# Sink keys in two transfers, limits and slopes on another queue, early weights one at a time

## The chip, the cores and the metric

The kernel runs on one core of a Trainium2 chip. The metric is the device time of one execution in microseconds (us). Engines: TensorE (PE), VectorE (DVE), ScalarE (ACT), GpSimd (POOL), and SyncE (SP), whose queue issues transfers.

## The reference

Windowed attention with a few always visible first keys ("sinks"), then two dense blocks on all 1536 rows:

```python
B, H, S, D = 2, 8, 768, 64              # n_sink = 4, window = 128
scores = q @ k.T / sqrt(D)
keep = (key < n_sink) | ((0 <= row - key) & (row - key < window))
a = softmax(where(keep, scores, -1e9))
x = (a @ v)                             # to [B*S, H*D] = [1536, 512]
x = (silu(x @ w_gate) * (x @ w_val)) @ w_out          # d_ff 1536
h = x @ w_in                                          # d_ff 2048
out = (max(h, 0) + alpha * min(h, 0)) @ moe2_w_out
```

`n_sink` and `window` are inputs, so the masks are built on the chip. All of it has to be accurate: each matmul of the dense blocks is three matmuls on a high and a low part.

## The kernel before, in words

Attention is cut into 24 groups (`Group`). A group is one sequence, two heads (a head pair, `hp`) and two blocks of 128 rows. The first eight groups (`ORDER`, `NPASS`) give the first 512 rows of x; none of them has a sink block apart from the window. The sixteen groups after them run beside the first experts' work. A group goes through stages: `load` (keys and queries, four transfers), `load_v` (values, two), `prep` (transposes on TensorE, ScalarE copies them to `th`), `scores` (matmuls; VectorE adds the mask and takes the bound `nb`; ScalarE takes the exponential and its sum), `norm` (VectorE the reciprocal `rinv`, GpSimd the product), `flip` (transposes of the probabilities), `values` (matmuls, and the split into xh and xl). `attention` (L364) writes these in software-pipelined order: iteration x has scores of group x, values of x-2, flip of x-1, norm of x, prep of x+2, load of x+3, load_v of x+1.

Ahead of iteration 0, `begin_a` builds the identity and loads `n_sink` and `window` (`limits`, L75), `begin_b` builds the masks and loads and prepares the slopes alpha (`slopes`, L92; 2048 single values of 4 bytes). At the end of iterations 0 and 1 `sink_load` (L350) asks for the first 32 keys of all heads of a sequence in four transfers, at the end of iterations 2 and 3 `sink_keys` (L358) transposes them into `kst`.

A group with sinks keeps the probabilities of a block as 128 window columns and 32 sink columns (`KW` = 160), with the sinks behind in the first block and ahead in the second. `norm` multiplies the window columns of both blocks in one GpSimd operation and the sinks in two, into `sk`, which a transpose (L320) turns for the value matmuls.

Expert weights come as 64-bit values, 512 KB a piece. `Stream.load` asks for one (three raw buffers, `RB`), `convert` makes a high and a low part with two ScalarE and four VectorE operations, and `tick` (L597) does one of each. While the first eight groups run, `tick` is called at the flips until two weights are converted (`EARLY`, L851); after that, one step of the first expert unit and one `tick` follow each 2300 units of attention's cost. The unit goes through the gate matmuls (pg), the value matmuls (pv) and the output matmuls (po).

The order in which instructions are written gives priorities; a planner with a simulated timeline then orders the instructions of each engine and each queue, and may draw one ahead when its engine would be idle. All transfers are issued on SP's queue, in order, and one issue waits there for its buffer to come free.

Of the kernel before, what the change touches and what calls it, by code (L numbers as in the profile page):

```python
# [16 lines left out]
P = 128  # L17
# [17 lines left out]
WB = 13  # L35
WX = 6
RB = 3
VB = 4
ORDER = ((0, 3), (1, 2), (4, 5))
EARLY = 2  # L40
WEAVE = 2300
NG = 2
# [32 lines left out]
def limits(nc, g, n_sink, window):  # L75
    lim = []
    for nm, src in (("ns", n_sink), ("wd", window)):
        raw = g.const.tile([P, 2], I32, name=nm + "_raw")
        nc.sync.dma_start(out=raw, in_=src.bitcast(I32).partition_broadcast(P))
        lo = g.const.tile([P, 1], F32, name=nm + "_lo")  # L80
        nc.vector.tensor_copy(lo, raw[:, 0:1].bitcast(U32))
        hi = g.const.tile([P, 1], F32, name=nm + "_hi")
        nc.vector.tensor_copy(hi, raw[:, 1:2])
        v = g.const.tile([P, 1], F32, name=nm + "_v")
        nc.vector.scalar_tensor_tensor(
            out=v, in0=hi, scalar=4294967296.0, in1=lo, op0=ALU.mult, op1=ALU.add
        )
        lim.append(v)
    g.ns, g.wd = lim


def slopes(nc, g, alpha):  # L92
    nc.sync.dma_start(out=g.alpha, in_=alpha.rearrange("(f p) -> p f", p=P))
    nc.vector.tensor_scalar(out=g.sig, in0=g.alpha, scalar1=1.0, scalar2=-2.0, op0=ALU.is_gt, op1=ALU.mult)
    nc.vector.tensor_scalar(out=g.sig, in0=g.sig, scalar1=1.0, scalar2=None, op0=ALU.add)
    nc.vector.tensor_tensor(out=g.sal, in0=g.alpha, in1=g.sig, op=ALU.mult)
    nc.vector.tensor_scalar(out=g.sdn, in0=g.sig, scalar1=DOWN, scalar2=None, op0=ALU.mult)
# [34 lines left out]
def attention_pools(nc, tc, ctx, g):  # L132
    for nm, bufs in (("raw_p", 2), ("tr_p", 3), ("pr_p", 3), ("pt_p", 2), ("st_p", 4)):
        setattr(g, nm, ctx.enter_context(tc.tile_pool(name=nm, bufs=bufs)))
    g.nb = g.const.tile([P, B * H * NQ], F32, name="nb")
    g.wsum = g.const.tile([P, NW], F32, name="wsum")
    g.ksr = [g.const.tile([NPAIR * SINK, 2 * D], F32, name="ksr") for _ in range(B)]
    g.kst = [g.const.tile([P, NPAIR * SINK], F32, name="kst") for _ in range(B)]
    g.vsr = g.const.tile([4 * SINK, NPAIR, NG, 2 * D], F32, name="vsr")
    nc.gpsimd.memset(g.vsr, 0.0)  # L140


class Group:
# [109 lines left out]
            )  # L253

    def prb_at(self, t):
        return 2 * self.blocks(0)[0] if t else 0

    def pr(self, t, e, c, n):
        w = self.blocks(t)[0]
# [3 lines left out]
    def norm(self):  # L263
        nc, g = self.nc, self.g
        rinv = g.st_p.tile([P, NG, 2], F32, tag="rinv", name="rinv")
        nc.vector.tensor_scalar(out=rinv, in0=self.ssum, scalar1=EPS, scalar2=None, op0=ALU.add)
        nc.vector.reciprocal(out=rinv, in_=rinv)
        for c, n, dst in ((0, P, None), (1, SINK, "sk")) if self.sink else ((None, 0, None),):
            if c is None:
                for t in range(NG):  # L270
                    w = self.blocks(t)[0]
                    o = self.prb_at(t)
                    v = self.prb[:, o:o + 2 * w].rearrange("p (e w) -> p e w", e=2)
                    r = rinv[:, t].unsqueeze(2).to_broadcast([P, 2, w])
                    nc.gpsimd.tensor_tensor(out=v, in0=v, in1=r, op=ALU.mult)
                continue
            offs = []
            for t in range(NG):
                w, blk, sp, kk = self.blocks(t)
                offs.append(self.prb_at(t) + (sp if c else blk[0]))  # L280
            step = offs[1] - offs[0]
            v = self.prb[:, offs[0]:offs[0] + 2 * step].rearrange("p (t w) -> p t w", t=NG)
            if step >= 2 * KW:
                v = v[:, :, :2 * KW].rearrange("p t (e w) -> p t e w", e=2)[:, :, :, :n]
                parts = [(v, slice(0, NG))]
            else:
                parts = [
                    (self.prb[:, o:o + 2 * KW].rearrange("p (t e w) -> p t e w", t=1, e=2)[:, :, :, :n], slice(t, t + 1))
                    for t, o in enumerate(offs)
                ]  # L290
            if dst:
                self.sk = g.pr_p.tile([P, NG, 2, SINK], F32, tag="sk", name="sk")
            for v, ts in parts:
                r = rinv[:, ts].unsqueeze(3).to_broadcast([P, ts.stop - ts.start, 2, n])
                nc.gpsimd.tensor_tensor(out=self.sk[:, ts] if dst else v, in0=v, in1=r, op=ALU.mult)

    def flip(self, t):
        nc, g = self.nc, self.g
        w, blk, sp, kk = self.blocks(t)
        if t == 0:  # L300
            self.pt = g.pt_p.tile([P, 2, 2 * NG, P], F32, tag="pt", name="pt")
        nb = len(blk)
        ps = g.ps_t.tile([P, 512], F32, tag="ps", name="ps_p")
        for e in range(2):
            for x, c in enumerate(blk):
                y = (e * nb + x) * P
                nc.tensor.transpose(ps[:, y:y + P], self.pr(t, e, c, P), g.ident)
        b0 = max(0, 2 * t - self.off)
        psv = ps[:, :2 * nb * P].rearrange("p (e c) -> p e c", e=2)
        if sp is None:  # L310
            nc.scalar.activation(self.pt[:, :, b0:b0 + nb].rearrange("p e a c -> p e (a c)"), psv, AF.Copy)
        else:
            nc.vector.tensor_tensor(
                out=self.pt[:, :, b0:b0 + 2], in0=psv.unsqueeze(2).to_broadcast([P, 2, 2, P]),
                in1=g.tri.unsqueeze(1).to_broadcast([P, 2, 2, P]), op=ALU.mult,
            )
        if t == NG - 1 and self.sink:
            self.pts = g.pt_p.tile([P, P], F32, tag="pts", name="pts")
            ps = g.ps_t.tile([P, 512], F32, tag="ps", name="ps_p2")
            nc.tensor.transpose(ps[:, 0:P], self.sk.rearrange("p t e s -> p (t e s)"), g.ident)  # L320
            nc.scalar.activation(self.pts, ps[:, 0:P], AF.Copy)

    def values(self):
# [24 lines left out]


def sink_load(nc, g, k, b):  # L350
    for hp in range(NPAIR):
        nc.sync.dma_start(
            out=g.ksr[b][hp * SINK:(hp + 1) * SINK].rearrange("p (e d) -> p e d", e=2),
            in_=k[b, 2 * hp:2 * hp + 2, 0:SINK, :].rearrange("h p d -> p h d"),
        )


def sink_keys(nc, g, b):  # L358
    ps = g.ps_t.tile([P, 512], F32, tag="ps", name="ps_ks")
    nc.tensor.transpose(ps[:, :P], g.ksr[b], g.ident)  # L360
    nc.scalar.activation(g.kst[b], ps[:, :P], AF.Copy)


def attention(groups, begin):  # L364
# [15 lines left out]
    for x in range(n + 2):  # L380
        if x < n:
            for t in range(NG):
                groups[x].scores(t)
            yield 1200, None
        if x >= 2:
            for c in groups[x - 2].values():
                yield c, None
            yield 0, groups[x - 2]
        if 1 <= x <= n:
            for t in range(NG):  # L390
                groups[x - 1].flip(t)
            yield 1000, None
        if x < n:
            groups[x].norm()
            yield 0, None
        if x + 2 < n:
            for c in groups[x + 2].prep():
                yield c, None
        stage("load", x + 3)
        stage("load_v", x + 1)  # L400
        if x < B:
            begin[2](x)
        elif x < 2 * B:
            begin[3](x - B)


def verdict(nc, g):
# [130 lines left out]
class Stream:  # L538
# [55 lines left out]
        self.w[i] = (wh, wl)  # L594
        self.n_conv += 1

    def tick(self):  # L597
        n = len(self.seq)
        if self.n_conv < n and self.room() and self.n_load > self.n_conv:
            self.convert()  # L600
        while self.n_load < n and self.n_load < self.n_conv + RB:
            self.load()

    def get(self, i):
# [201 lines left out]
def fast(nc, tc, ctx, g, n_sink, window, alpha, q, k, v, w_gate, w_val, w_out, x2_in, x2_out, out):  # L806
# [5 lines left out]
    m1, m2 = moe(nc, g, st, xs, out, [[blk * NG * P for blk in pair] for pair in ORDER])  # L812

    def begin_a():
        identities(nc, g)
        limits(nc, g, n_sink, window)

    def begin_b():
        masks(nc, g)
        slopes(nc, g, alpha)  # L820

    with ExitStack() as inner:
        attention_pools(nc, tc, inner, g)
# [18 lines left out]
        per = len(groups) // NPASS  # L842
        ready = []
        done = cost = 0
        for c, grp in attention(groups, (begin_a, begin_b, lambda b: sink_load(nc, g, k, b), lambda b: sink_keys(nc, g, b))):
            cost += c
            if grp is not None:
                done += 1
# [1 line left out]
                    ready.append(m1.unit(0, done // per - 1))  # L850
            if done < per:  # L851
                if c == 1000 and st.n_conv < EARLY:
                    st.tick()
            elif cost >= WEAVE:
                cost -= WEAVE
                while ready and next(ready[0], ready) is ready:
                    ready.pop(0)
                st.tick()
# [66 lines left out]
```

## Time and profile before

| what | us |
| --- | --- |
| median of 3 runs | 691.95 |
| lowest, highest | 690.81, 693.9 |
| profiled execution, its own time | 690.96 |
| span of its profile | 689.2 |
| TensorE busy | 660.7 |
| VectorE busy | 405.7 |
| ScalarE busy | 301.4 |
| GpSimd busy | 50.5 |

The span reaches from the first to the last instruction that the profile shows; the execution's own time has some 1.8 us around it. TensorE's matmuls are pipelined, so its busy time is a share of the span in which some matmul was under way. In the profile, "idle before" names how long an engine did nothing ahead of an instruction, and what ended that.

### The profile page before, as it was taken

What the parts mean: (1) busy time and instruction counts of PE and PEld (TensorE: products, weight loads), DVE (VectorE), ACT (ScalarE), POOL (GpSimd) and SP (SyncE); (2) the same over time, 40 slices, a digit from 0 to 9 for tenths busy, and PEclk for the clock granted to TensorE, in tenths of its full rate; (3) what the DMA queues carried; (4) which work ended last, traced back from release to release, by engine and by line L of the source; (5) the groups of instructions that cost most, each with busy time, mean ns of one, the idle gap of its engine ahead of it and who ended that gap; (6) DMA issues with size and microseconds to landing.
All of it is one profiled execution on the core that took longest, in us unless ns stands there. A gap on an engine that the chain in (4) does not pass through costs nothing.

```text
span 689.2 us, 9053 instructions
## 1 busy us (share of the span) xinstructions
PE 660.7 (96%) x3195; PEld 527.6 (77%) x3195; DVE 405.7 (59%) x926; ACT 301.4 (44%) x686; POOL 50.5 (7%) x98
## 2 busy tenths in 40 slices
PE   5599999999999999999999999999999999999996
PEld 3366767677678888888888888888888888888885
DVE  4687778656379852379642599427933844333432
ACT  4787866565266622054422365436612532113320
POOL 2342113411100000000000000000000000000000
PEclk9899999999999999999999999999999999999999
DMA  4858455321025530033400043201400000000111
GB/s 91 222 121 216 141 147 117 86 58 23 1 91 175 173 112 0 1 104 115 149 0 1 0 153 118 97 1 61 154 31 0 1 0 1 1 0 1 61 62 66
DMA packets 76772, 50.88 MB, mean 74 GB/s; under 512 B 51120, under 2 KB 71600, under 8 KB 76720
## 3 DMA queue, kind: packets, MB, share of 16 engines
q1 hardware_dynamic: 76720, 50.23, 25.4%
q8 instruction: 27, 0.44, 0.3%
q14 instruction: 25, 0.20, 0.1%
HBM read 47.07 MB, written 3.15 MB: 73 GB/s over the span
## 4 chain that ended last, share of the span: by engine, by line
PE 86%; DVE 5%; ACT 3%; DMA 3%; issue 1%; SPq 1%; POOL 0%; DVEq 0%; ACTq 0%; POOLq 0%
PE ph L646 6%; PE pf L770 6%; PE ph L644 6%; PE pf L768 6%; PE pf L769 6%; PE ph L645 6%; PE po L712 5%; PE po L714 5%; PE po L713 5%; PE pg L644 4%; PE pv L644 4%; PE pg L645 4%; PE pv L646 4%; PE pg L646 4%; PE pv L645 4%; PE ps_s L240 2%
## 5 line engine op out<-in xcount | busy, mean ns | idle before, releaser
L657 ACT ACTIVATE hh<-hid 128x512 fp32r<-128x512 f32 x84 | 53.0, 631 | 74.8 <-DVE hid L696 43.7
L658 DVE TENSOR_TENSOR hl<-hid,hh 128x512 fp32r<-128x512 f32 x84 | 57.8, 688 | 31.5 <-ACT hh L657 31.5
L750 ACT ACTIVATE neg<-ph,sal 128x512 f32<-128x512 f32 x48 | 33.0, 687 | 96.8 <-PE ph L646 96.7
L644 PE MATMUL ph<-yh,wh 128*128 128x512 f32 x192 | 74.8, 389 | 0.0
L646 PE MATMUL ph<-yh,wl 128*128 128x512 f32 x192 | 74.7, 389 | 0.0
L645 PE MATMUL ph<-yl,wh 128*128 128x512 f32 x192 | 74.7, 389 | 0.0
L768 PE MATMUL pf<-wh,hh 128*128 128x512 f32 x192 | 74.7, 389 | 0.0
L769 PE MATMUL pf<-wl,hh 128*128 128x512 f32 x192 | 74.7, 389 | 0.0
L770 PE MATMUL pf<-wh,hl 128*128 128x512 f32 x192 | 72.4, 389 | 0.0
L592 ACT ACTIVATE wh<-w_m 128x512 fp32r<-128x512 f32 x68 | 42.7, 631 | 52.0 <-DVE w_m L583 18.4
L593 DVE TENSOR_TENSOR wl<-w_m,wh 128x512 fp32r<-128x512 f32 x68 | 48.1, 710 | 24.5 <-ACT wh L592 23.9
L752 DVE SCALAR_TENSOR_TENSOR hid<-ph,sig,neg 128x512 f32<-128x512 f32 x48 | 36.0, 749 | 39.6 <-ACT neg L750 39.3
L712 PE MATMUL po<-hh,wh 128*128 128x512 f32 x144 | 56.9, 396 | 1.9 <-ACT hh L657 1.2
L644 PE MATMUL pg<-xh,wh 128*128 128x512 f32 x144 | 56.8, 397 | 0.7 <-ACT pr L250 0.7
L644 PE MATMUL pv<-xh,wh 128*128 128x512 f32 x144 | 56.6, 393 | 0.0
L645 PE MATMUL pg<-xl,wh 128*128 128x512 f32 x144 | 56.2, 390 | 0.0
L713 PE MATMUL po<-hh,wl 128*128 128x512 f32 x144 | 56.1, 390 | 0.0
L646 PE MATMUL pg<-xh,wl 128*128 128x512 f32 x144 | 56.1, 390 | 0.0
L646 PE MATMUL pv<-xh,wl 128*128 128x512 f32 x144 | 56.1, 390 | 0.0
L645 PE MATMUL pv<-xl,wh 128*128 128x512 f32 x144 | 56.0, 389 | 0.0
L775 DVE TENSOR_TENSOR acc<-pf,acc 128x512 f32<-128x512 f32 x36 | 23.2, 686 | 50.5 <-PE pf L770 50.5
L714 PE MATMUL po<-hl,wh 128*128 128x512 f32 x144 | 52.7, 392 | 0.0
(123 smaller groups left out, 1202.8 us busy)
## 6 DMA issues: line engine op xcount, KB each, us to landing
w_raw<-in_moe_w_out SPq DMA_DIRECT2D x28, 512.0 KB, 3.3
w_raw<-in_moe_w_in SPq DMA_DIRECT2D x16, 512.0 KB, 3.7
w_raw<-in_moe_w_gate SPq DMA_DIRECT2D x12, 512.0 KB, 3.9
w_raw<-in_moe_w_val SPq DMA_DIRECT2D x12, 512.0 KB, 4.2
qr<-in_q SPq DMA_DIRECT2D x48, 64.0 KB, 2.4
vr<-in_v SPq DMA_DIRECT2D x32, 96.0 KB, 2.4
out<-acc SPq DMA_DIRECT2D x12, 256.0 KB, 2.2
kr<-in_k SPq DMA_DIRECT2D x32, 64.0 KB, 2.3
```

The costliest lines, as they stand in the source:

```text
L593: nc.vector.tensor_tensor(out=wl, in0=w32, in1=wh, op=ALU.subtract)
L644: nc.tensor.matmul(ps, wh[:, c], xh[:, kk], start=(kk == 0), stop=False)
L645: nc.tensor.matmul(ps, wh[:, c], xl[:, kk], start=False, stop=False)
L646: nc.tensor.matmul(ps, wl[:, c], xh[:, kk], start=False, stop=(kk == KD - 1))
L657: nc.scalar.activation(hh, hid, AF.Copy)
L658: nc.vector.tensor_tensor(out=hl, in0=hid, in1=hh, op=ALU.subtract)
L712: nc.tensor.matmul(ps, wh[:, mc], hh, start=(x == 0), stop=False)
L713: nc.tensor.matmul(ps, wl[:, mc], hh, start=False, stop=False)
L714: nc.tensor.matmul(ps, wh[:, mc], hl, start=False, stop=(x == CHUNK - 1))
L768: nc.tensor.matmul(ps, hh[:, ts], wh, start=(x == 0), stop=False)
L769: nc.tensor.matmul(ps, hh[:, ts], wl, start=False, stop=False)
L770: nc.tensor.matmul(ps, hl[:, ts], wh, start=False, stop=(x == CHUNK - 1))
```

## The change

- The transfers of `n_sink`, `window` and alpha are issued on ScalarE's queue; `limits` is written ahead of the identities.
- `sink_load` has two transfers for a sequence, one for each head of the pairs, into one buffer for both sequences. The first sequence's is written at the end of `begin_b`; at the end of iteration 2 the first is transposed and the second asked for; at the end of iteration 4 the second is transposed.
- `tick` takes the number of raw weights that may be ahead: one in the first ticks, two once more than one group is done, three as before later on.
- There are three value buffers (`VB`) in place of four.
- The second block's probabilities of a group with sinks lie 128 columns further on, so that all four sink parts stand 160 columns apart, and one GpSimd operation normalises them.

```diff
-VB = 4
+VB = 3
@@ limits, slopes
-        nc.sync.dma_start(out=raw, in_=src.bitcast(I32).partition_broadcast(P))
+        nc.scalar.dma_start(out=raw, in_=src.bitcast(I32).partition_broadcast(P))
-    nc.sync.dma_start(out=g.alpha, in_=alpha.rearrange("(f p) -> p f", p=P))
+    nc.scalar.dma_start(out=g.alpha, in_=alpha.rearrange("(f p) -> p f", p=P))
@@ Group
     def prb_at(self, t):
-        return 2 * self.blocks(0)[0] if t else 0
+        return (P + 2 * KW if self.sink else 2 * P) if t else 0
@@ norm, with sinks
+        self.sk = g.pr_p.tile([P, NG * 2, SINK], F32, tag="sk", name="sk")
+        s0 = self.blocks(0)[2]
+        v = self.prb[:, s0:s0 + 4 * KW].rearrange("p (x w) -> p x w", w=KW)[:, :, 0:SINK]
+        r = rinv.rearrange("p t e -> p (t e)").unsqueeze(2).to_broadcast([P, 2 * NG, SINK])
+        o = self.prb_at(1) + self.blocks(1)[1][0]
+        w = self.prb[:, :]
+        u = bass.AP(tensor=w.tensor, offset=w.offset, ap=[list(w.ap[0]), [o, NG], [KW, 2], [1, P]])
+        nc.gpsimd.tensor_tensor(out=u, in0=u, in1=rinv.unsqueeze(3).to_broadcast([P, NG, 2, P]), op=ALU.mult)
+        nc.gpsimd.tensor_tensor(out=self.sk, in0=v, in1=r, op=ALU.mult)
@@ sink_load
-    for hp in range(NPAIR):
-        nc.sync.dma_start(
-            out=g.ksr[b][hp * SINK:(hp + 1) * SINK].rearrange("p (e d) -> p e d", e=2),
-            in_=k[b, 2 * hp:2 * hp + 2, 0:SINK, :].rearrange("h p d -> p h d"),
-        )
+    g.ksr = g.raw_p.tile([NPAIR * SINK, 2 * D], F32, tag="ksr", name="ksr", bufs=1)
+    kv = k[b].rearrange("(hp e) s d -> e hp s d", e=2)
+    for e in range(2):
+        nc.sync.dma_start(out=g.ksr[:, e * D:(e + 1) * D], in_=kv[e, :, 0:SINK, :])
@@ attention, end of iteration x
-        if x < B:
-            begin[2](x)
-        elif x < 2 * B:
-            begin[3](x - B)
+        if x in (2, 4):
+            begin[2](x // 2 - 1)
@@ Stream
-    def tick(self):
+    def tick(self, ahead=RB):
-        while self.n_load < n and self.n_load < self.n_conv + RB:
+        while self.n_load < n and self.n_load < self.n_conv + ahead:
@@ fast
     def begin_a():
+        limits(nc, g, n_sink, window)
         identities(nc, g)
-        limits(nc, g, n_sink, window)
     def begin_b():
         masks(nc, g)
         slopes(nc, g, alpha)
+        sink_load(nc, g, k, 0)
+    def begin_c(b):
+        sink_keys(nc, g, b)
+        if b + 1 < B:
+            sink_load(nc, g, k, b + 1)
-                    st.tick()
+                    st.tick(1 + (done > 1))
```

## Rows read from the trace of the kernel before

**Rows 1.** Busy us by stretch: PE, PEld, DVE, ACT, POOL; granted clock, DMA share, GB/s.
```profile
20.00:30.00 10.00, 4.43 (x35) 2.78 (x33) 9.05 (x27) 9.40 (x33) 3.03 (x4) 0.95 0.81 190
...
10.00:54.50 44.50, 34.47 (x226) 22.19 (x224) 32.24 (x128) 35.77 (x123) 16.93 (x24) 0.92 0.66 163
...
60.00:70.00 10.00, 10.00 (x50) 7.73 (x49) 9.58 (x18) 7.31 (x15) 2.20 (x3) 1.00 0.70 198
...
54.00:124.00 70.00, 65.94 (x394) 48.94 (x391) 55.43 (x173) 46.58 (x133) 17.22 (x36) 1.00 0.57 153
124.00:689.00 565.00, 556.98 (x2572) 454.63 (x2570) 313.94 (x598) 216.88 (x430) 14.47 (x31) 1.00 0.18 57
```

**Rows 2.** TensorE's waits: total us, times, longest.
```profile
PE ps_k L204 <- DMA kr<-in_k: 10.2, 4, 4.0
```

**Rows 3.** Chain of waits, first 60 us: start, us, what.
```profile
6.79 3.59 DMA alpha<-in_moe_alpha
...
17.95 5.17 DMA kr<-in_k
```

**Rows 4.** Timeline 0 to 14 us: start, us, engine, line, instruction, idle before.
```profile
2.76 0.47 SPq L79 DMA_DIRECT2D ns_raw<-in_n_sink  x1
...
5.26 0.60 ACT L209 ACTIVATE th<-ps_k 128x512 f32<-128x512 f32 x1 [3.24 <-PE ps_k L204]
...
6.64 0.15 DVE L81 CAST wd_lo<-wd_raw 128x1 f32<-128x1 uint32 x1 [0.77 <-DMA wd_raw<-in_window]
...
7.37 1.00 SPq L171 DMA_DIRECT2D kr<-in_k  x1
...
7.41 0.69 PE L204 MATMUL ps_k<-ident,kr 128*128 128x128 f32 x2 [2.19 <-DMA kr<-in_k]
...
8.47 0.58 SPq L172 DMA_DIRECT2D qr<-in_q  x1
...
9.31 0.29 DVE L246 CUSTOM_DVE_ANT_0 ps_s<-ps_s,mask 128x128 f32<-128x128 f32 x1
...
13.05 0.17 DVE L266 TENSOR_SCALAR rinv<-ssum 128x4 f32<-128x4 f32 x1 [1.19 <-ACT pr L250]
```

**Rows 5.** Timeline 13 to 34 us, the same columns.
```profile
13.19 1.88 SPq L352 DMA_DIRECT2D ksr<-in_k  x4
...
15.11 1.53 SPq L555 DMA_DIRECT2D w_raw<-in_moe_w_gate  x3
...
23.22 0.41 PE L204 MATMUL ps_k<-ident,kr 128*128 128x128 f32 x2 [2.81 <-DMA kr<-in_k]
...
26.16 1.83 SPq L352 DMA_DIRECT2D ksr<-in_k  x4
...
31.45 0.45 PE L360 MATMUL ps_ks<-ident,ksr 128*128 128x128 f32 x1 [4.20 <-DMA ksr<-in_k]
...
33.10 0.37 ACT L250 ACTIVATE pr<-ps_s,nb 128x128 f32<-128x128 f32 x1 [2.46 <-DVE nb L246]
```

**Rows 6.** Timeline 51 to 66 us: weights, first expert matmuls, conversions' last operation.
```profile
51.35 1.50 SPq L555 DMA_DIRECT2D w_raw<-in_moe_w_val  x3
...
54.55 0.50 PE L644 MATMUL pg<-xh,wh 128*128 128x512 f32 x1
...
61.72 0.39 PE L644 MATMUL pv<-xh,wh 128*128 128x512 f32 x1
...
62.00 0.68 DVE L593 TENSOR_TENSOR wl<-w_m,wh 128x512 fp32r<-128x512 f32 x1
...
65.48 0.78 DVE L593 TENSOR_TENSOR wl<-w_m,wh 128x512 fp32r<-128x512 f32 x1
```

**Rows 7.** Line 295 by form: duration ns min, median, max; first and last start.
```profile
L295 POOL TENSOR_TENSOR sk<-pr,rinv x32: 293/296/766, 54.2 to 181.2; 128x64 f32<-128x64 f32 x32
```

**Rows 8.** DMA issues: count, KB each, median us from issue to landing.
```profile
vr<-in_v SPq DMA_DIRECT2D x32, 96.0 KB, 2.4
...
ksr<-in_k SPq DMA_DIRECT2D x8, 16.0 KB, 2.8
```

More of the change, by code (lines that the diff above doesn't have):

```diff
@@ L136, in attention_pools @@
     g.wsum = g.const.tile([P, NW], F32, name="wsum")
-    g.ksr = [g.const.tile([NPAIR * SINK, 2 * D], F32, name="ksr") for _ in range(B)]
     g.kst = [g.const.tile([P, NPAIR * SINK], F32, name="kst") for _ in range(B)]
@@ L267, in norm @@
         nc.vector.reciprocal(out=rinv, in_=rinv)
[L268 to L277, printed above, removed]
-            for t in range(NG):
[L279 to L295, printed above, removed]
@@ new lines, in norm @@
+        if not self.sink:
+            for t in range(NG):
+                w = self.blocks(t)[0]
+                o = self.prb_at(t)
+                v = self.prb[:, o:o + 2 * w].rearrange("p (e w) -> p e w", e=2)
+                nc.gpsimd.tensor_tensor(out=v, in0=v, in1=rinv[:, t].unsqueeze(2).to_broadcast([P, 2, w]), op=ALU.mult)
+            return
+        self.sk = g.pr_p.tile([P, NG * 2, SINK], F32, tag="sk", name="sk")
+        s0 = self.blocks(0)[2]
+        v = self.prb[:, s0:s0 + 4 * KW].rearrange("p (x w) -> p x w", w=KW)[:, :, 0:SINK]
@@ L319, in flip @@
             ps = g.ps_t.tile([P, 512], F32, tag="ps", name="ps_p2")
-            nc.tensor.transpose(ps[:, 0:P], self.sk.rearrange("p t e s -> p (t e s)"), g.ident)
+            nc.tensor.transpose(ps[:, 0:P], self.sk.rearrange("p x s -> p (x s)"), g.ident)
             nc.scalar.activation(self.pts, ps[:, 0:P], AF.Copy)
@@ L350, in sink_load @@
 def sink_load(nc, g, k, b):
-    for hp in range(NPAIR):
-        nc.sync.dma_start(
-            out=g.ksr[b][hp * SINK:(hp + 1) * SINK].rearrange("p (e d) -> p e d", e=2),
-            in_=k[b, 2 * hp:2 * hp + 2, 0:SINK, :].rearrange("h p d -> p h d"),
-        )
+    g.ksr = g.raw_p.tile([NPAIR * SINK, 2 * D], F32, tag="ksr", name="ksr", bufs=1)
+    kv = k[b].rearrange("(hp e) s d -> e hp s d", e=2)
+    for e in range(2):
+        nc.sync.dma_start(out=g.ksr[:, e * D:(e + 1) * D], in_=kv[e, :, 0:SINK, :])
 def sink_keys(nc, g, b):
     ps = g.ps_t.tile([P, 512], F32, tag="ps", name="ps_ks")
-    nc.tensor.transpose(ps[:, :P], g.ksr[b], g.ident)
+    nc.tensor.transpose(ps[:, :P], g.ksr, g.ident)
     nc.scalar.activation(g.kst[b], ps[:, :P], AF.Copy)
@@ L844, in fast @@
         done = cost = 0
-        for c, grp in attention(groups, (begin_a, begin_b, lambda b: sink_load(nc, g, k, b), lambda b: sink_keys(nc, g, b))):
+        for c, grp in attention(groups, (begin_a, begin_b, begin_c)):
             cost += c
```

## The prediction, made before the changed kernel was run

> **What bounds the kernel now.** I read the busy time by stretches first, then TensorE's waits, the chain of waits, and last the timeline around each hole. From 124 us on, TensorE is busy 557.0 of 565 us, and from 54 to 124 us 65.9 of 70 [rows 1]: what comes after the first expert matmul at 54.55 us [rows 6] is a fixed amount of matmul work, some 634 us, that starts when that matmul starts. So the change is worth what it takes off the first 54.5 us, less what it adds behind them. In that stretch TensorE has two kinds of holes: it waited for keys four times, 10.2 us [rows 2], and once for raw sink keys, 4.20 us [rows 5]. The chain of waits runs through the same transfers: the slopes (alpha) from 6.79 us, and keys that took 5.17 us from 17.95 us [rows 3]. But TensorE's holes are not all to be won. ScalarE is busy 35.8 of the 44.5 us from 10 to 54.5 [rows 1], and in 20 to 30 us, around the second hole, 9.40 of 10: there it converted early weights while TensorE waited. A TensorE hole that ScalarE fills comes back as ScalarE work later. All of ScalarE's idle time from 10 us on is 8.7 us; no gain there is above that.
>
> **The change part by part.** The sum is made against the profiled execution, 690.96 us (span 689.2 and 1.76 around it), which is 0.99 us under the median of the runs, 691.95; the difference found is then taken from the median.
>
> (a) *Limits and slopes off SP's queue.* An issue on SP takes 0.47 us. SP loses three before the loads of the third group; the two sink issues that now stand there give two back. The window limit reaches VectorE at 6.64 us [rows 4] and the first mask lands on scores at 9.31. Asked for on ScalarE's queue from 0.74 us, as ScalarE's second issue, it starts some 2.0 us earlier (it was the sixth issue on SP, from about 3.25; now about 1.25), and the mask chain (2.67 us from 6.64 to 9.31) could end at 7.3. TensorE's first scores stand behind the second group's keys, which it waited for until 7.41; two issues less ahead of them bring that to 6.5, the first scores to about 7.1, the first mask to about 7.7: 1.6 us won. The second pair of scores of the first group stood on VectorE behind the slopes, which landed 3.59 us after 6.79; that goes too, so the normaliser at 13.05 can come at about 10.5, 2.5 us earlier. The second group's scores stand behind the third group's loads, one net issue earlier on SP (0.5) and no longer right behind the slopes, where one issue took 1.00 and the next 0.58 in place of 0.47 each (0.6): 1.1 us. Bounds 1.1 and 2.6; I take 2.0, as the normaliser is what releases the first flips. ScalarE pays three issues (1.4 us) before its table load, in a stretch where it does nothing else until 5.26 [rows 4]; if that cover failed, it would cost up to 1.4. On the new queue the slopes' transfer runs beside the first groups' loads. The Trainium skill ("DMA: Bandwidth & Descriptors", Issuing engines are not separate DMA queues) says that transfers asked for by different engines run on the same 16 DMA engines and interleave, so that only the issuing time is saved. By that rule the 0.6 us of slow issues would not go but move to the second group's loads, and (a) would be 1.4 and the sum 0.6 us less; no run so far shows a transfer on ScalarE's queue.
>
> (b) *Early weights one at a time, sink loads out of the middle.* Before the fifth group's loads SP issued four sink transfers (1.88 us) and three weights of 512 KB (1.53 us) [rows 5]; the keys then shared the DMA engines with 1.5 MB and took 5.17 us, where a value load of 96 KB has a median of 2.4 [rows 8]. After the change SP has one weight there and no sink issue: 1.88 and about 1.0 us less on SP, and landing near 2.5 us. TensorE's hole of 2.81 us at 23.22 [rows 5] should close. Bounds: 2.8 if ScalarE follows, 0.5 if only ScalarE's idle time goes (it was idle 0.6 of 10 us there). I take 1.0, nearer ScalarE's row, since it is the busier engine there.
>
> (c) *Sink keys asked for in two transfers, two iterations ahead of their transposition.* TensorE's hole of 4.20 us at 31.45 is the second sequence's: issued from 26.16 to 27.99 [rows 5], transposed one iteration after, and the next scores stand behind it in TensorE's order. Now the second sequence is asked for behind x = 2 and transposed behind x = 4. With iterations of about 4 us (the first eight groups need some 42 us in all) that leaves 8 us for a landing of 2.8 [rows 8]. ScalarE was idle 2.46 us of this hole, so the bounds are 2.46 and 4.20; I take 3.0, nearer ScalarE's row, since ScalarE has the whole group's work to do behind it. Next late here is ScalarE.
>
> (d) *One raw weight fewer on its way.* Before, five weights were asked for before the experts' first matmul (three, one, one), now four (one, one, two). The fifth, the first of the value matrix, can only be asked for with the next batch, at 51.35 us before. The one that led that batch was fully converted at 62.68 (62.00 + 0.68) [rows 6], 11.3 us after its issue; the first value matmul came at 61.72. So the fifth weight would be a good 1 us late, and every conversion behind it moves by one place, 3.48 us (62.00 to 65.48), in a stretch in which VectorE is busy 9.58 of 10 us. Bounds 0 (attention matmuls fill the hole) and 3.5; I take a loss of 1.5, between them, since attention groups have matmuls to put there but the conversions are VectorE's.
>
> (e) *Sinks normalised in one operation.* Two GpSimd operations of 0.295 us become one of twice the size [rows 7], between 0.30 and 0.59 us: at most 0.3 us for each of 16 groups, on an engine that waits for VectorE's normalisers. It comes after the larger operation, on which the flips wait, as before: 0, bounds 0 and a gain of 0.5. If GpSimd were the bound, it would be 16 x 0.3.
>
> (f) *Three value buffers for four.* A value load now waits for the value matmuls of the same iteration, ahead of it in TensorE's order, and is used three iterations later, over 12 us against 2.4 for the transfer [rows 8]: 0, bounds 0 and a loss of 1.0 through loads and weights queued behind it on SP, since the queue is in order.
>
> Sum: -2.0 - 1.0 - 3.0 + 1.5 = -4.5 us: 686.5 by the profile, 691.95 - 4.5 = 687.4 by the median.
>
> **The rivals.** *ScalarE takes the place of the holes.* The start's 2.0 us stay, the sink hole gives 1.0 and the keys' 0.5, and (d) takes 1.5: -2.0, 690.0 us. For it: the 9.40 of 10 us. Against it: ScalarE's 2.46 us of idleness lie in the sink hole itself. *The hole stays.* The order on TensorE is planned, and a transposition may again be put before its transfer lands; then (c) gives nothing: -1.5, 690.4. For it: two transfers of the same size in place of four, sharing the queue with weights; against it: two iterations in place of one. The Trainium skill (same page, Why a DMA increments its semaphore by 16 and not by 1) says that the number of DMA engines is the largest up to 16 that divides the outermost sizes of both sides; the new source has 4 head pairs outermost, so it would run on 4 engines. By that a sink transfer of 128 rows would load each of four engines with 32, where a key load of 256 rows gives each of 16 only 16: an estimate that favours this rival, which no run so far shows. *Weights late (the slower side).* Place: the first expert unit. If not one but three conversions slip behind the first expert matmul, since raw weights come one at a time, that is 3 x 3.48 = 10.4 us against the 6.0 won: +4.4, 696.4. It decides from 6.0 / 3.48 = 1.7 conversions on. For it: VectorE's 9.58 of 10. Against it: before, five were converted in the front's gaps, and four can still be there. *All holes go*, with ScalarE's conversions fitted in: -2.0 - 2.8 - 4.2 + 1.5 = -7.5, 684.4.
>
> **How the numbers follow.** Forecast 0.45, ScalarE 0.20, the hole stays 0.13, weights late 0.12, all holes 0.10. The range 683.6 to 693.0 holds the forecast with the ends of (a) to (d), the first two rivals and the best case, and leaves out most of the slower one. About 0.5%, 3.5 us, is what a measurement can tell here: below 688.5 is faster. Three quarters of the forecast, the best case and some of the two small rivals make 0.54; most of the slower rival 0.10; the rest, 0.36, is no change.
>
> **What would show it.** Right, step by step: the first expert matmul near 48.5 us in place of 54.55; the first mask under 8 us and the normaliser near 11; no wait of TensorE for keys near 20 us and none for sink keys; weights issued one by one before 25 us; the first value matmul's weight converted about when it is needed. Wrong: the first expert matmul still after 52 us (ScalarE or a new transfer holds it), or holes over 2 us among the first value or output matmuls.

## The result and the profile after

The changed kernel takes 699.94 us (median of 4 runs, 698.83 to 700.4) against 692.55 for the kernel before beside it: ratio 1.0118, 95% interval 1.0098 to 1.0138. It is about 8 us slower (7.4 by the medians, 8.2 by the ratio), outside the range given. The profiled execution took 699.78 us, its span is 698.0.

The view by stretches again (the columns of [rows 1]); the first fence is the changed kernel, the second adds a stretch of the kernel before.

```profile
20.00:30.00 10.00, 8.51 (x59) 5.92 (x55) 9.48 (x38) 9.66 (x36) 1.82 (x3) 0.88 0.79 212
...
13.00:67.16 54.16, 40.79 (x222) 26.21 (x220) 45.39 (x138) 41.77 (x135) 17.25 (x22) 0.78 0.74 201
67.16:124.00 56.84, 55.59 (x323) 42.42 (x321) 34.26 (x118) 30.91 (x90) 11.19 (x21) 1.00 0.36 94
...
124.00:698.00 574.00, 565.30 (x2635) 460.73 (x2634) 321.66 (x632) 221.78 (x451) 16.16 (x30) 1.00 0.19 58
```

```profile
13.00:54.55 41.55, 32.83 (x221) 21.52 (x221) 30.86 (x120) 33.78 (x115) 16.98 (x24) 0.92 0.67 166
```

67.16 and 54.55 us are the first expert matmul of the two kernels. From 13 us to it, ScalarE has 8.0 us more work (41.8 against 33.8) and VectorE 14.5 (45.4 against 30.9), and ScalarE's idle time grows from 7.8 to 12.4. The work is weight conversions: 13 have started on ScalarE before the first expert matmul, 5 in the kernel before. Behind it there is less of them to do: from 67.16 to 124 TensorE is idle 1.3 us, where it was idle 4.1 in the 70 us of [rows 1]. TensorE has almost the same number of matmul records in the two stretches (222 and 221), but is busy 40.8 us with them in place of 32.8, and idle 13.4 in place of 8.7. So of the 12.6 us by which the stretch is longer, 8.0 are longer busy time for as many matmuls and 4.7 are more waiting (the ends of matmuls are modelled in the profile, so the split is rough).

TensorE's waits (idle time in us, times, the longest one) and the start of the timeline of the changed kernel, beside [rows 2, 4]; the last fence has the first keys of the kernel before:

```profile
PE ps_k L203 <- DMA kr<-in_k: 7.8, 2, 7.1
PE ps_s L239 <- ACT pr L249: 5.0, 5, 2.3
```

```profile
0.74 0.42 ACTq L79 DMA_DIRECT2D ns_raw<-in_n_sink  x1
...
1.68 0.46 ACTq L93 DMA_DIRECT2D alpha<-in_moe_alpha  x1
...
5.32 0.15 DVE L81 CAST wd_lo<-wd_raw 128x1 f32<-128x1 uint32 x1 [1.09 <-DMA wd_raw<-in_window]
...
7.11 0.66 PE L203 MATMUL ps_k<-ident,kr 128*128 128x128 f32 x2 [7.11 <-DMA kr<-in_k]
...
9.80 0.30 DVE L245 CUSTOM_DVE_ANT_0 ps_s<-ps_s,mask 128x128 f32<-128x128 f32 x1 [0.66 <-PE ps_s L239]
...
12.72 0.17 DVE L265 TENSOR_SCALAR rinv<-ssum 128x4 f32<-128x4 f32 x1 [1.19 <-ACT pr L249]
```

```profile
3.98 0.66 PE L204 MATMUL ps_k<-ident,kr 128*128 128x128 f32 x2 [3.98 <-DMA kr<-in_k]
```

The limits came 1.3 us earlier (5.32 against 6.64), but the first keys 3.1 us later (7.11 against 3.98), so the first mask lands on the scores 0.5 us later (9.80 against 9.31) and the first normaliser is only 0.33 us earlier than in [rows 4]. Apart from this first wait the holes that were to go are gone: 0.7 us of waiting for keys is left, and the sink keys cost no wait. Now the middle, beside [rows 5, 6]:

```profile
32.95 0.42 PE L346 MATMUL ps_ks<-ident,ksr 128*128 128x128 f32 x1
...
35.26 0.93 SPq L539 DMA_DIRECT2D w_raw<-in_moe_w_val  x2
...
36.36 0.35 ACT L249 ACTIVATE pr<-ps_s,nb 128x128 f32<-128x128 f32 x1
...
36.95 0.20 ACT L249 ACTIVATION_READ_ACCUMULATOR pr<-ps_s,nb 128x1 f32 x1
39.02 0.66 ACT L559 ACTIVATE w_m<-w_raw 128x512 f32<-128x512 f32 x1 [1.87 <-DMA w_raw<-in_moe_w_val]
39.58 0.19 ACT L559 ACTIVATION_READ_ACCUMULATOR w_m<-w_raw 128x1 f32 x1
39.67 0.46 ACT L249 ACTIVATE pr<-ps_s,nb 128x256 f32<-128x256 f32 x1
40.02 0.19 ACT L249 ACTIVATION_READ_ACCUMULATOR pr<-ps_s,nb 128x1 f32 x1
40.63 0.67 ACT L559 ACTIVATE w_m<-w_raw 128x512 f32<-128x512 f32 x1 [0.42 <-DMA w_raw<-in_moe_w_val]
41.20 0.19 ACT L559 ACTIVATION_READ_ACCUMULATOR w_m<-w_raw 128x1 f32 x1
41.30 0.46 ACT L249 ACTIVATE pr<-ps_s,nb 128x256 f32<-128x256 f32 x1
...
45.84 0.36 ACT L249 ACTIVATE pr<-ps_s,nb 128x128 f32<-128x128 f32 x1
...
37.44 0.14 DVE L245 DVE_READ_ACCUMULATOR2_ANT nb<- 128x1 f32 x1
...
40.27 0.48 PE L239 MATMUL ps_s<-th 64*128 64x128 f32 x2 [2.28 <-ACT pr L249]
41.90 1.33 PE L239 MATMUL ps_s<-th 64*128 64x256 f32 x4 [1.15 <-ACT pr L249]
...
67.16 0.50 PE L628 MATMUL pg<-xh,wh 128*128 128x512 f32 x1
...
74.92 0.39 PE L628 MATMUL pv<-xh,wh 128*128 128x512 f32 x1
```

This is the loss seen from close by. The fifth and the sixth weight, values, are asked for at 35.26 us, 16 us ahead of the batch in [rows 6], and their conversions stand in ScalarE's order between the exponentials of one attention group. ScalarE does not pass a conversion that waits: it stands 1.87 us until the raw weight has landed, and the group's exponential, whose input VectorE had ready at 37.6 (37.44 + 0.14), comes at 39.67. TensorE's next scores wait 2.28 us for it, and 1.15 us in the same way behind the next weight. The exponentials of the groups show what goes with conversions among them. Start of the first exponential of groups 5 to 9 in us, and in brackets the conversions that start between it and that of the group before:

| kernel | 5 | 6 | 7 | 8 | 9 |
| --- | --- | --- | --- | --- | --- |
| before | 33.10 | 38.46 (1) | 43.22 (0) | 46.82 (0) | 50.37 (0) |
| changed | 29.28 | 36.36 (1) | 45.84 (3) | 51.56 (1) | 61.74 (3) |
| after_x13, below | 29.34 | 33.58 (1) | 37.75 (0) | 41.83 (0) | 49.44 (2) |

At group 5 the changed kernel is 3.8 us ahead, of the 6.0 that (a), (b) and (c) were to give by then. From there a group with three conversions takes 9.5 and 10.2 us, one with two 7.6, one with none 3.6 to 4.8 in these three kernels (q_only, below, has one with none of 6.9). From 45 us on TensorE is also at the lower of its clocks; in the stretch before, 36 to 46 us, it was busy 5.97 of 10 us:

```profile
45.00:50.00 5.00, 3.89 (x16) 2.92 (x15) 4.58 (x16) 3.61 (x15) 1.66 (x2) 0.50 0.98 288
50.00:55.00 5.00, 3.49 (x16) 1.66 (x15) 4.37 (x15) 4.56 (x16) 2.34 (x4) 0.50 0.79 208
55.00:60.00 5.00, 4.98 (x20) 3.29 (x22) 4.89 (x9) 3.04 (x8) 2.27 (x3) 0.50 0.60 173
```

A granted clock of 0.50 is 1.2 GHz, for 15 us. In its last 5 us TensorE is busy 4.98, so there its own matmuls hold it up and no wait does. VectorE, too, is nearly full in these 15 us, 13.8 busy, with the work of the conversions. The conversions ahead thus come with three things, exponentials that stand behind them, a nearly full VectorE and a slow TensorE; what part of the loss each makes, no run separates.

### The profile page after: what moved, and what is told of

Same layout as the page of the kernel before. It is cut to its first block, busy times and chain, and to the rows that moved or that the text cites. A ratio compares the mean times of both kernels' runs of the same rounds, so it can differ in the third digit from the quotient of the medians.

```text
span 698.0 us, 9033 instructions
## 1 busy us (share of the span) xinstructions
PE 666.9 (96%) x3195; PEld 532.2 (76%) x3195; DVE 407.3 (58%) x926; ACT 298.7 (43%) x684; POOL 46.9 (7%) x82
## 4 chain that ended last, share of the span: by engine, by line
PE 87%; DVE 5%; DMA 3%; ACT 2%; issue 1%; SPq 1%; POOL 0%; DVEq 0%; ACTq 0%; POOLq 0%
PE ph L630 6%; PE pf L754 6%; PE ph L629 6%; PE pf L753 6%; PE pf L752 6%; PE ph L628 6%; PE po L696 5%; PE po L698 5%; PE pv L628 5%; PE pg L628 5%; PE pv L630 5%; PE po L697 5%; PE pv L629 5%; PE pg L629 5%; PE pg L630 5%; PE xp L325 2%
## 5 line engine op out<-in xcount | busy, mean ns | idle before, releaser
L642 DVE TENSOR_TENSOR hl<-hid,hh 128x512 fp32r<-128x512 f32 x84 | 58.2, 692 | 32.8 <-ACT hh L641 32.8
L577 DVE TENSOR_TENSOR wl<-w_m,wh 128x512 fp32r<-128x512 f32 x68 | 48.5, 716 | 23.8 <-ACT wh L576 23.2
```

The costliest lines, as they stand in the source:

```text
L577: nc.vector.tensor_tensor(out=wl, in0=w32, in1=wh, op=ALU.subtract)
L642: nc.vector.tensor_tensor(out=hl, in0=hid, in1=hh, op=ALU.subtract)
```

## The experiments

Fifteen runs; the times are medians beside the kernel before on the same chip, the ratios with their 95% intervals. The first question was which part does it.

**no_tick**: the change without the early weights one at a time.

```diff
-                    st.tick(1 + (done > 1))
+                    st.tick()
...
```

> The changed kernel with the early weights asked for three at a time again; everything else of the change stays. Theory 1 (conversions drawn ahead: in the changed kernel 13 weight conversions start on ScalarE before the first expert matmul against 5 before, and that matmul moved from 54.55 to 67.16 us): with the old tick the planned order has 10 conversions ahead of the first Silu in place of 14 (8 in the kernel before), so the first expert matmul comes near 58 us and the time near 693 (691 to 695). Theory 2 (the transfers on ScalarE's queue, first keys at 7.11 in place of 3.98 us): the start is unchanged, time near 699. Theory 3 (three value buffers): unchanged, 699.

687.45 us, 0.9946 (0.9929 to 0.9963). The loss is gone, as theory 1 had it, but the sizes were missed: the kernel is 4 us faster than before, not 1 to 2 us slower, and the first expert matmul, at 54.30 with 8 conversions ahead, 4 us earlier than expected. Theories 2 and 3, which had 699, fall.

**no_sink**: the change with the old sink transfers.

```diff
-        if x in (2, 4):
-            begin[2](x // 2 - 1)
+        if x < B:
+            begin[2](x)
+        elif x < 2 * B:
+            begin[3](x - B)
...
```

> The changed kernel with the sink keys as before (four transfers, at the end of iterations 0 and 1); everything else of the change stays. Theory 1: 9 conversions ahead of the first Silu, first expert matmul near 56 us, time near 692 (690 to 694.5). Theories 2 and 3: 699. If the order of the sinks themselves cost the time, also a drop, but with 13 conversions still ahead of the first expert matmul.

689.42, 0.9980 (0.9966 to 0.9994), first expert matmul 57.22, 7 conversions ahead; the time is a little under theory 1's 690 to 694.5. So in the changed kernel the loss needs both parts.

**alpha_sp**: only the slopes back on SP's queue.

```diff
-    nc.scalar.dma_start(out=g.alpha, in_=alpha.rearrange("(f p) -> p f", p=P))
+    nc.sync.dma_start(out=g.alpha, in_=alpha.rearrange("(f p) -> p f", p=P))
```

> The changed kernel with the slopes' transfer back on SP's queue, the two limits still on ScalarE's; the planned order of the conversions is that of the changed kernel. Theory 1: the first keys land near 4.0 us again, but the loss lies in the conversions: first expert matmul still after 64 us, time 697 to 700. Theory 2: the late first keys (3.1 us) and what follows are the loss: time 692 to 695.

699.35, 1.0120 (1.0103 to 1.0137). The first keys came at 5.43 us, not at 4.0: the limits alone delay them by 1.4. But the loss is all there, so theory 2 falls.

**early8**: the kernel before, with more conversions in the first groups.

```diff
-EARLY = 2
+EARLY = 8
```

> The kernel before with one edit: EARLY = 8 in place of 2, so the early ticks convert up to eight weights at the flips of the first groups (11 conversions in the planned order ahead of the first Silu in place of 8). Nothing of the change is in it. Theory 1: each further conversion ahead costs 1.1 us net (8.8 us for 8): 3 more, near 696 (694.5 to 698), first expert matmul near 59 us. Theories 2 and 3: no slower than 692.5, since the conversions have to be made in any case and come away from the busy stretch behind 54 us.

689.32, 0.9977 (0.9957 to 0.9997), first expert matmul 56.04, 9 conversions ahead, at most one in a group from the fourth on. Theory 1, a fixed price for each conversion ahead, falls: four more cost 1.5 us ahead of the first expert matmul and save 3.5 behind it.

**st** and **t_only**: the two parts together, and the weights alone, on the kernel before.

```diff
+    def tick(self, ahead=RB):
+                    st.tick(1 + (done > 1))
# st only, with the two transfers of sink_load:
+        if x in (2, 4):
+            begin[2](x // 2 - 1)
...
```

> The kernel before with two parts of the change alone: the sink keys in two transfers asked for later, and the early weights one at a time. Limits and slopes stay on SP's queue, four value buffers, sinks normalised in two operations. Theory A (the two parts together, through the planned order, draw conversions into the first groups: 14 ahead of the first Silu in the planned order; in the changed kernel a group with three conversions took 9.5 and 10.2 us where one with none took 3.6): 12 or 13 conversions ahead of the first expert matmul, that matmul after 63 us, time 696 to 700. Rival (the loss needs the transfers on ScalarE's queue, the value buffers or the sinks' operation): near 688.

700.64, 1.0134 (1.0106 to 1.0162), as theory A had it within 0.7 us; 12 conversions ahead:

```profile
68.71 0.80 PE L640 MATMUL pg<-xh,wh 128*128 128x512 f32 x1
```

> The kernel before with the early weights one at a time alone. Planned order: 7 conversions ahead of the first Silu (8 before). Theory A: no conversions in bunches in the first eight groups, time 688 to 694, first expert matmul near 54 us or earlier. Rival (asking for the weights one at a time costs the time by itself, the weights being late): 696 to 700, with waits for raw weights.

688.67, 0.9954 (0.9939 to 0.9970); 4 conversions ahead, first expert matmul 52.56. Two parts, each of which makes the kernel faster (the sinks alone stand below), make it 1.3% slower together, and nothing else of the change is needed.

**gate_after**: the changed kernel, conversions 5 to 11 held back.

```diff
         nc.vector.reciprocal(out=rinv, in_=rinv)
+        if len(g.gate) < 10:
+            t = g.const.tile([P, 1], F32, name="gate")
+            nc.vector.tensor_scalar(out=t, in0=rinv[:, 0, 0:1], scalar1=0.0, scalar2=None, op0=ALU.mult)
+            g.gate.append(t)
...
-            nc.scalar.activation(m, hi.bitcast(F32), AF.Abs, scale=scale, accum_out=g.wsum[:, slot:slot + 1])
+            j = 7 if 5 <= i < 12 else -1
+            b = {'bias': g.gate[j]} if 0 <= j < len(g.gate) else {}
+            nc.scalar.activation(m, hi.bitcast(F32), AF.Abs, scale=scale, accum_out=g.wsum[:, slot:slot + 1], **b)
```

> The changed kernel with one addition: the conversions of weights 5 to 11 take as bias a zero that is made from the normaliser of the eighth group (one tiny VectorE operation for each of ten groups), so they can't start before it. Requests of weights, sinks, queues and buffers stay as changed. Theory A: 5 conversions ahead of the eighth group's normaliser, first expert matmul at 53 to 57 us in place of 67.2, time 687 to 692. Rival (the late keys at the start, or the transfers and buffers, hold the first groups): first expert matmul after 62 us, 696 to 700.

693.70, 1.0040 (1.0029 to 1.0051). The first expert matmul is 12.1 us earlier, as theory A had it:

```profile
55.06 0.50 PE L635 MATMUL pg<-xh,wh 128*128 128x512 f32 x1
```

The time missed the expectation, because what lies behind takes 637.2 us in place of 630.8: 7 conversions are made ahead in place of 13, and from there to 124 us TensorE is idle 6.8 us. Why that is more than in the kernel before, which has only 5 ahead and 634.7 behind, stays open.

**gl0_sp**: a try at a better kernel, with the conversions held back one by one (bias=g.gate[i]) and slopes asked for at the end of iteration 10.

> Put together from the theory: the change without the early weights one at a time and with four value buffers, the slopes asked for on SP at the end of iteration 10 in place of the start, and conversions 2 to 11 each held back to the normaliser of the group of the same number (about one for a group). Theory A: first keys near 4 us, first normaliser near 11 us in place of 13.05, 8 or 9 conversions ahead of the first expert matmul at 50 to 54 us, time 683 to 687. Rival (VectorE and ScalarE are the bound of the first groups, an earlier start is lost in them): 687 to 690.

693.25, 1.0030 (1.0014 to 1.0045): a miss. The first keys came at 5.44, not at 4.0, with the limits still on ScalarE's queue. The first normaliser came at 10.96, 2.1 us early, but nothing of it was left at the first expert matmul (60.85); TensorE waited 8.4 us for GpSimd's products, 1.0 in the kernel before. As the conversions are held as well, the run doesn't show what the early start alone is worth.

**nq, s_only, q_only, no_vb**: single parts. nq is no_tick with limits and slopes on SP; s_only and q_only are one part alone on the kernel before; no_vb is the changed kernel with VB = 4.

```diff
# no_vb
-VB = 3
+VB = 4
```

> The change without the early weights one at a time and with limits and slopes on SP's queue as before: sinks in two transfers asked for later, three value buffers, sinks normalised in one operation. The planned order of conversions is that of the run no_tick (10 ahead of the first Silu), which differs from it only by the queue of limits and slopes and measured 687.45. Theory A (small transfers on ScalarE's queue delay the first keys by 3.1 us, which the masks' earlier end takes back to some 0.3 us): first keys near 4 us, first expert matmul 53 to 55 us, time 686 to 688. Rival (the predicted gain of the queue, 2.0 us): 689 to 690.

688.14, 0.9956 (0.9941 to 0.9972), against no_tick's 0.9946: no difference that the intervals show. First keys 4.20, first normaliser 13.22.

> The kernel before with the sink keys in two transfers asked for later, alone (9 conversions ahead of the first Silu in the planned order, 8 before). Theory A: TensorE's 4.2 us wait for sink keys at 31.45 us goes, first expert matmul 1 to 3 us earlier than 54.55, time 686.5 to 689.5, as the prediction's step (c) had it (-3.0). Rival (the groups are bound by ScalarE and VectorE, or the hole moves): 690 to 692.

689.47, 0.9975 (0.9963 to 0.9987): 1.7 us faster, and the wait for sink keys is gone. But the first expert matmul is not earlier, as theory A had it, it is 2.3 us later:

```profile
56.89 0.80 PE L640 MATMUL pg<-xh,wh 128*128 128x512 f32 x1
```

The gain lies behind it: 631.0 us there in place of 634.7, with 7 conversions ahead in place of 5.

> The kernel before with limits and slopes on ScalarE's queue and the limits written ahead, alone (9 conversions ahead of the first Silu). Theory A: first keys at 7.0 us in place of 4.0, first normaliser within 0.5 us of 13.05, time 690 to 692.5: no change. The prediction's step (a): normaliser near 11, time near 689.

689.80, 0.9982 (0.9968 to 0.9996), keys at 7.11, normaliser at 12.73: about 1 us faster, half of what step (a) had. Here, too, the first expert matmul is later (55.47), and the gain lies behind it.

> The changed kernel with four value buffers again. 14 conversions ahead of the first Silu, as in the changed kernel. Theory A: no change, 698.5 to 701. Rival (the third buffer's loss holds SP's queue): 691 to 696.

700.03, 1.0128 (1.0107 to 1.0149): the third value buffer has no part in it.

What was left open: whether the two parts cost the time, or only the order that the planner made of them. The order can be counted: conversions planned on ScalarE ahead of the first Silu, ScalarE's first operation on the expert unit. The traces have the same counts.

```text
before 8, early weights one at a time alone 7, sinks alone 9, both 14, changed 14
changed, sinks transposed one iteration earlier (1 and 3) 8
changed, two raw weights ahead in all early ticks 8
```

**after_x13, after_tick2, stnv_tick2**: all parts of the change stay, one number differs.

```diff
# after_x13
-        if x in (2, 4):
-            begin[2](x // 2 - 1)
+        if x in (1, 3):
+            begin[2]((x - 1) // 2)
...
# after_tick2; stnv_tick2 is the same with limits and slopes on SP
-                    st.tick(1 + (done > 1))
+                    st.tick(2)
```

> The whole changed kernel with one edit: the sink keys are transposed (and the second sequence's asked for) at the end of iterations 1 and 3 in place of 2 and 4. Every part of the change is in it; the planned order has 8 conversions ahead of the first Silu in place of 14. Theory A (the bunches in the planned order cost the time, not the two parts): first expert matmul at 52 to 57 us, time 686.5 to 690. Rival (the later sinks and the single early weights cost it themselves): 697 to 700, as the kernel changed by one iteration.

685.35, 0.9916 (0.9898 to 0.9935): 2.0% under the changed kernel, 14 us, and the lowest ratio of all.

> The whole changed kernel with one edit: two raw weights may be ahead in all early ticks, in place of one in the first two. 8 conversions ahead of the first Silu in the planned order. Theory A: first expert matmul at 52 to 57 us, time 686.5 to 690. Rival: 697 to 700.

686.75, 0.9943 (0.9925 to 0.9962).

> The run after_tick2 with limits and slopes on SP's queue as before; the planned order of conversions and weights is the same. First keys near 4 us in place of 7. Theory A: within 1.0 us of after_tick2 (the queue's effect on the first normaliser is some 0.3 us). Rival (the prediction's step (a)): 2.0 us slower than after_tick2.

687.09, 0.9952 (0.9933 to 0.9971): with this plan of conversions, the queue of limits and slopes makes no difference that can be measured.

The timeline of after_x13, for comparison with the fence on the middle above, its stretch up to the first expert matmul and that from 36 to 46 us, then the latter of the changed kernel:

```profile
39.93 0.37 SPq L539 DMA_DIRECT2D w_raw<-in_moe_w_val  x1
...
43.63 0.70 ACT L559 ACTIVATE w_m<-w_raw 128x512 f32<-128x512 f32 x1 [1.34 <-DMA w_raw<-in_moe_w_val]
...
53.21 0.50 PE L628 MATMUL pg<-xh,wh 128*128 128x512 f32 x1
...
13.00:53.21 40.21, 32.22 (x222) 21.44 (x218) 31.08 (x118) 34.10 (x119) 15.40 (x22) 0.96 0.78 198
...
36.00:46.00 10.00, 8.60 (x64) 5.85 (x63) 7.49 (x29) 8.10 (x29) 4.27 (x8) 1.00 0.68 168
```

```profile
36.00:46.00 10.00, 5.97 (x33) 3.34 (x30) 7.47 (x23) 7.16 (x22) 2.28 (x3) 0.84 0.85 230
```

In the 10 us from 36 to 46 VectorE is as busy in both, and ScalarE even less busy in the slow one, so that full engines don't explain 64 matmul records against 33 there; the waits behind the conversions, read above, fit it. The DMA engines carry more in the slow one (0.85 against 0.68), and if that made the raw weights later was not tested. In the whole stretch up to the first expert matmul after_x13 has the same 222 matmul records as the changed kernel, with TensorE busy 32.2 us and idle 8.0, against 40.8 and 13.4. All runs in one table, from their profiles: first expert matmul, conversions started on ScalarE before it, and the rest of the span behind it.

| run | conversions | first expert matmul | rest |
| --- | --- | --- | --- |
| t_only | 4 | 52.56 | 634.5 |
| before | 5 | 54.55 | 634.7 |
| stnv_tick2, after_tick2 | 7, 7 | 51.92, 52.07 | 632.8, 632.7 |
| after_x13 | 7 | 53.21 | 631.5 |
| gate_after | 7 | 55.06 | 637.2 |
| q_only, s_only, no_sink | 7, 7, 7 | 55.47, 56.89, 57.22 | 632.1, 631.0, 632.4 |
| no_tick, nq | 8, 8 | 54.30, 54.95 | 631.6, 631.4 |
| early8, gl0_sp | 9, 9 | 56.04, 60.85 | 631.2, 630.4 |
| st, no_vb | 12, 12 | 68.71, 69.26 | 629.8, 629.6 |
| changed, alpha_sp | 13, 13 | 67.16, 67.70 | 630.8, 630.4 |

Up to 9 conversions ahead the first expert matmul lies between 52 and 61 us, with 12 or 13 between 67 and 69. The rest behind it takes 634.7 us with 5 ahead, 630.4 to 632.8 with 7 to 9 (gate_after, 637.2, apart) and 629.6 to 630.8 with 12 or 13. So a few conversions ahead pay, and the others gain little behind and cost more ahead.

## Why the prediction was wrong

The step that failed is (d), and with it the sum, which added the parts as if the order of the instructions stayed. (d) said that the fifth weight "can only be asked for with the next batch", and saw the risk in conversions that come late. The planner asked for it at 35.26 us and drew conversions in among the first groups, 13 ahead of the first expert matmul in place of 5. The first expert matmul came 12.6 us later and the rest behind it took 3.8 us less, +8.8 by the profiles in place of the -4.5 of the sum. The price of the early weights in the changed kernel is the distance to no_tick, 1.0118 against 0.9946: some 12 us in place of 1.5.

The slower rival had the direction and half of the price (+4.4), but another place (the first expert unit; the loss lies in the groups ahead of it) and the opposite mechanism: the weights came too early, not too late. The argument against it, that conversions fill gaps in the front, took the gaps as free; [rows 1] showed ScalarE busy 9.40 of 10 us there.

The premise that what follows the first expert matmul is a fixed 634 us did not hold either: it took 629.6 to 637.2. The signs that the prediction named came out so: first expert matmul 67.16 in place of 48.5, first mask 9.80 in place of under 8, normaliser 12.72 in place of 11, but no wait for keys near 20 us and none for sink keys.

- (a) predicted -2.0. The window limit came 1.3 us earlier, but the first keys were 3.1 us late, which the sum didn't have: the normaliser is 0.33 us earlier. q_only measured some -1.2 (0.9982 of 691), nq against no_tick and stnv_tick2 against after_tick2 no difference. The rule of the Trainium skill ("DMA: Bandwidth & Descriptors", Issuing engines are not separate DMA queues) is that transfers of several queues run on the same engines and interleave. The trace agrees in that transfers on ScalarE's queue held up those on SP's; that they interleave, it doesn't show. The price was not the 0.6 us put on it but some 1.4 us of delay for the first keys by the limits (5.43 with them alone) and 1.7 more by the slopes.
- (b) right in its mechanism: the hole at 23.22 is gone. With the weights one at a time alone, (b) and (d) together were to be +0.5 and measured -3.2 (t_only, 0.9954 of 691, without the sinks' share of (b)).
- (c) half right. No wait for sink keys is left in the runs that have it, but the closed hole did not bring the first expert matmul forward: in s_only it came 2.3 us later, and the -1.7 (in place of -3.0) lie behind it. The iterations were taken as 4 us where 42 us for eight groups make 5.3, which only leaves the transfer more time.
- (e) 32 operations of 0.30 us became 16 of 0.40; no run has this part alone. (f) right: no_vb differs by nothing.
- Parts with -3.2 and -1.7 alone gave +9.3 together (st, 1.0134). With the plan put right (after_x13) all parts together give -5.8 us, 0.9916. That this is near the -4.5 of the sum is in part luck: the first expert matmul comes 1.3 us earlier, not 6.0, and the rest takes 3.2 us less, which the sum took as fixed.

Why the planner leaves its old order when both parts are there was not settled: in the planned orders alone, one iteration in the sinks' place or one weight more in two ticks is enough for 14 or 8.

## What to carry to other kernels

Where a planner orders the instructions, a small edit can change the whole order; count in the planned order what has moved across the stage that sets the end before adding up single savings, and try neighbouring values of the edited number. Work drawn ahead into an early stage is free only as far as that stage has gaps for it, and here an instruction that waited for a transfer stopped everything behind it on its engine. Two good parts are to be measured together and apart.

## What had not been expected of the hardware

Two transfers of 1 KB and one of 8 KB in 2048 pieces on a second queue delayed the first keys, 64 KB asked for at the same moments, from about 4.0 us (3.79 to 4.39 in the seven profiles without them) to 5.43 and 5.44 with the limits and 7.0 to 7.1 with the slopes as well. Where the transfers held each other up is not shown. From 3 to 4 us the DMA engines were busy 0.57 in the kernel before and only 0.09 in the changed one, so there the keys did not wait for full engines; from 5 to 6 us the share was 1.43 in the changed kernel, at 144 GB/s (columns of [rows 1], the kernel before first).

```profile
3.00:4.00 1.00, 0.03 (x1) 0.06 (x1) 0.00 (x0) 0.00 (x0) 0.00 (x0) 1.00 0.57 126
```

```profile
3.00:4.00 1.00, 0.00 (x0) 0.00 (x0) 0.58 (x6) 0.45 (x1) 0.00 (x0) 1.00 0.09 16
...
5.00:6.00 1.00, 0.00 (x0) 0.00 (x0) 0.68 (x7) 0.00 (x0) 0.00 (x0) 1.00 1.43 144
```
